# One searched round of 92 single steps, a second transpose bank, and FFN output in the FFN input's banks

## The chip, the cores and the metric

The kernel runs on one core of a Trainium2 chip. The metric is the device time in microseconds (us). The time of the kernel before is 358.19 us (median of 2 runs, 357.36 to 359.02). PE is the TensorE, DVE the VectorE, ACT the ScalarE, POOL the GpSimd, SP the engine that issues most DMA here. A program on one core has no second die to compare with, so "slow" below only means that a run was over 1.5% above the fastest run of the same kernel.

## The reference, cut to what matters

A recurrent attention (state 40x40 for each of 4x8 heads, 768 steps) feeds a feed-forward layer with a squared ReLU.

```
for t in range(S):
    y[:, :, t] = einsum('bhd,bhde->bhe', rt, state)
    Sa = einsum('bhde,bhe->bhd', state, at)
    state = state * wt[:, :, None, :] - einsum('bhd,bhe->bhde', Sa, bt) + einsum('bhd,bhe->bhde', vt, kt)
x = y.transpose(0, 2, 1, 3).reshape(B * S, H * D)        # 3072 x 320
h = x @ w_in;  r = maximum(h, 0);  out = (r * r) @ w_out   # 320 -> 2048 -> 320
```

The kernel works in 12 chunks of 64 time steps. In each round of its main loop it does three things at once: the recurrence of chunk c, the preparation (logs, scalings, transposes) of chunk c+1, and the feed-forward layer of chunks c-1 and c-2.

## The kernel before: the parts that matter

The kernel before shares out eight banks of PSUM like this: `hp` two (FFN input and cumulative sums), `acc` two (one buffer), `sq` two (one buffer), `tr` **one** (all transposes), `op2` one (FFN output). A helper makes the transposes and copies them out of PSUM at once. Most other steps too are a product with its evacuation right behind it:

```
def transposes(srcs, dst, eng):
    trp = ps.tile([128, 8, 128], BF16, name="trp", tag="tr", bufs=1)
    for i, s in enumerate(srcs):
        nc.tensor.transpose(out=trp[:, i, :], in_=s, identity=IDb[:])
    if eng == "act":
        nc.scalar.activation(out=dst, in_=trp[:], func=ACTF.Copy)
    else:
        nc.vector.tensor_copy(out=dst, in_=trp[:])

def g0(self, bp):          # product, then its evacuation on ACT
    self.pairs(self.accm[bp], self.PNT[bp], self.vm_of(self.VM, bp), not self.first)
    self.evac_m(bp, self.G0)
```

The main loop, cut (`cur` is chunk c, `nxt` c+1, `prv` c-1, `old` c-2):

```
for c in range(NCH):
    cur.a_s0(0); cur.pn(1); cur.g0(0)
    nxt.cs(0); nxt.cs(1); nxt.gamp(); prv.t_x()
    ...
    old.ffn_out(1, 0); cur.m(0); nxt.scale_b(); nxt.scale_k(); nxt.decays(); old.ffn_out(1, 1)
    cur.state(0); cur.t_vm(0, "dve"); nxt.scale_a()
    ...
    prv.ffn_in(0); prv.ffn_in(1); cur.a_s0(1); cur.cx(0); cur.g0(1)
    prv.ffn_in(2); nxt.t_r(); cur.t_s(0, nxt); cur.m(1); nxt.spread()
    prv.ffn_in(3); prv.ffn_in(4); cur.state(1); cur.t_vm(1, "dve"); nxt.t_kb(0)
    prv.ffn_in(5); cur.r_s0(0); cur.cx(1); cur.y(0); nxt.t_kb(1)
    prv.ffn_in(6); nxt.t_a(); cur.t_s(1, nxt); prv.ffn_in(7)
    ...
```

The program is scheduled by hand: each engine gets its own instructions in the order of this text and does not leave it.

Of the kernel before, what the change touches and what calls it, by code (L numbers as in the profile page):

```python
# [14 lines left out]
def kernel(  # L15
# [109 lines left out]
    def load(c, nat):  # L125
        for key, src in (("W", w), ("B", b), ("K", k), ("A", a)):
            t_ = ld.tile([128, NI, D], FP32, name=f"N{key}", tag=f"N{key}")
            for b2 in range(2):
                nc.sync.dma_start(out=t_[64 * b2:64 * b2 + 64], in_=src_view(src, c, b2))  # L129
            nat[key] = t_  # L130
# [17 lines left out]
    def transposes(srcs, dst, eng):  # L148
        trp = ps.tile([128, 8, 128], BF16, name="trp", tag="tr", bufs=1)
        for i, s in enumerate(srcs):  # L150
            nc.tensor.transpose(out=trp[:, i, :], in_=s, identity=IDb[:])  # L151
        if eng == "act":
            nc.scalar.activation(out=dst, in_=trp[:], func=ACTF.Copy)  # L153
        else:
            nc.vector.tensor_copy(out=dst, in_=trp[:])  # L155
# [5 lines left out]
    class Chunk:  # L161


        def __init__(self, c):
            self.c, self.nat = c, {}
            self.first, self.last = c == 0, c == NCH - 1
            i = c % 2
            self.Ap, self.Rp, self.Kp, self.Bp = Aps[i], Rps[i], Kps[i], Bps[i]
            self.VM = VMs[i]
            self.G0, self.Y = G0s[i], Ys[i]  # L170
            self.S, self.Sn = Ss[1 - i], Ss[i]
            self.ST, self.STn = {}, {}
            self.PNT, self.CXT, self.VMT, self.accm, self.accy = {}, {}, {}, {}, {}


        def ln(self):
# [4 lines left out]
            self.CSE = pr.tile([128, W_], FP32, name="CSE", tag="CSE", bufs=1)  # L181
            self.GAMI = pr.tile([128, W_], FP32, name="GAMI", tag="GAMI", bufs=1)

        def cs(self, j):
            cs = ps.tile([128, 512], FP32, name="cs", tag="hp", bufs=2)
            sl = slice(320 * j, 320 * j + 320)
            nc.tensor.matmul(out=cs[:, 0:320], lhsT=UTI[:], rhs=self.lnW[:, sl],  # L187
                             start=True, stop=True)
            nc.scalar.activation(out=self.GAMI[:, sl], in_=cs[:, 0:320], func=ACTF.Exp,  # L189
                                 scale=-1.0)  # L190
            nc.vector.tensor_tensor(out=self.CSE[:, sl], in0=cs[:, 0:320],  # L191
                                    in1=self.lnW[:, sl], op=ALU.subtract)
# [5 lines left out]
        def decays(self):  # L198
            GAMb = pr.tile([128, W_], BF16, name="GAMb", tag="GAMb", bufs=1)
            nc.gpsimd.tensor_tensor(out=GAMb[:], in0=self.GAMP[:],  # L200
# [3 lines left out]
            self.GLr = pr.tile([128, 4, 2, 160], BF16, name="GLr", tag="GLr")  # L204
            self.gld = dr.tile([2, W_], BF16, name="gld", tag="gld")
            for b2 in range(2):
                nc.gpsimd.dma_start(out=self.gld[b2:b2 + 1, :],
                                    in_=GAMb[64 * b2 + 63:64 * b2 + 64, :])

        def spread(self):  # L210
            for b2 in range(2):
# [13 lines left out]
        def scale_b(self):  # L225
            self.KB = pr.tile([128, 2, NI, 64], BF16, name="KB", tag="KB")
            self.scale("B", self.Bp, self.GAMI)
# [4 lines left out]
        def scale_k(self):  # L232
            self.scale("K", self.Kp, self.GAMI)
            for b2 in range(2):
# [7 lines left out]
        def t_r(self):  # L242
            self.RT = pr.tile([128, NG, 128], BF16, name="RT", tag="RT")
            transposes([self.Rp[:, 2 * g:2 * g + 2, :] for g in range(NG)], self.RT[:], "act")

        def t_kb(self, b2):
            if b2 == 0:
                self.KBT = pr.tile([128, 2, NG, 128], BF16, name="KBT", tag="KBT")
            transposes([self.KB[:, b2, 2 * g:2 * g + 2, :] for g in range(NG)],
                       self.KBT[:, b2], "act")  # L250

        def t_a(self):
            self.AT = pr.tile([128, NG, 128], BF16, name="AT", tag="AT")
            transposes([self.Ap[:, 2 * g:2 * g + 2, :] for g in range(NG)], self.AT[:], "act")


        def squares(self, lhs_of, rhs_of, dst):
# [3 lines left out]
            for g in range(4):  # L261
                for b2 in range(2):
                    for x in range(2):
                        mm(sq[:, x, g, b2, :], lhs_of(g, b2, 64 * x), rhs_of(g, b2, 64 * x),
                           True)
            nc.vector.tensor_tensor(  # L266
                out=dst[:].rearrange("s x g b t -> s (x g b) t"),
                in0=sq[:].rearrange("s x g b t -> s (x g b) t"),
                in1=MASK[:].to_broadcast([128, 16, L]), op=ALU.mult)

        def pn(self, bp):
            self.PNT[bp] = wk.tile([128, 2, 4, 2, L], BF16, name="PNT", tag="PNT")
            self.squares(lambda g, b2, r0: self.KBT[r0:r0 + D, b2, 4 * bp + g, :],
                         lambda g, b2, r0: self.AT[r0:r0 + D, 4 * bp + g,
                                                   64 * b2:64 * b2 + 64],
                         self.PNT[bp])

        def cx(self, bp):
            self.CXT[bp] = wk.tile([128, 2, 4, 2, L], BF16, name="CXT", tag="CXT")
            self.squares(lambda g, b2, r0: self.VMT[bp][r0:r0 + D, g, b2, :],  # L280
                         lambda g, b2, r0: self.RT[r0:r0 + D, 4 * bp + g,
                                                   64 * b2:64 * b2 + 64],
                         self.CXT[bp])
# [4 lines left out]
        def a_s0(self, bp):  # L288

            acc = self.accm[bp] = self.new_acc()  # L290
# [9 lines left out]
        def r_s0(self, bp):  # L300

            acc = self.accy[bp] = self.new_acc()
# [24 lines left out]
        def evac_m(self, bp, dst):  # L327
            for b2 in range(2):
                rows = slice(64 * b2, 64 * b2 + 64)
                src = self.accm[bp][rows, :, 0:320].rearrange(  # L330
# [6 lines left out]
        def g0(self, bp):  # L337
            self.pairs(self.accm[bp], self.PNT[bp], self.vm_of(self.VM, bp), not self.first)
            self.evac_m(bp, self.G0)

        def m(self, bp):
            self.pairs(self.accm[bp], self.PNT[bp], self.vm_of(self.G0, bp), True)
            self.evac_m(bp, self.VM)

        def state(self, bp):
# [3 lines left out]
            accs = self.new_acc()  # L349
# [5 lines left out]
            for z in range(2):  # L355
                for b2 in range(2):
                    for q in range(2):
# [4 lines left out]
                           kb[:, 2 * bp + q, :, z, 0:D], self.first and g == 0)  # L362
            for p in range(2):
# [10 lines left out]
        def t_s(self, bp, nxt):  # L374
            if self.last:
                return
            trs = ps.tile([128, 4, 2, 64], BF16, name="trs", tag="tr", bufs=1)
            for g in range(4):
                b2, q = divmod(g, 2)
                nc.tensor.transpose(out=trs[:, g].rearrange("s p d -> s (p d)"),  # L380
                                    in_=self.Sn[:, bp, b2, q].rearrange("s z e -> s (z e)"),
                                    identity=IDb[:])

            ST = nxt.ST[bp] = wk.tile([128, 2, 2, 2, D], BF16, name="ST", tag=f"ST{bp}")
            nc.vector.tensor_copy(out=ST[:].rearrange("s b q p d -> s (b q) p d"),  # L385
                                  in_=trs[:, :, :, 0:D])

        def t_vm(self, bp, eng):
            self.VMT[bp] = wk.tile([128, 4, 2, 128], BF16, name="VMT", tag="VMT")
            transposes([self.VM[:, b2, 8 * bp + 2 * g:8 * bp + 2 * g + 2, :]  # L390
                        for g in range(4) for b2 in range(2)],
                       self.VMT[bp][:].rearrange("s g b t -> s (g b) t"), eng)

        def y(self, bp):
            accy = self.accy[bp]
            self.pairs(accy, self.CXT[bp], self.kb_of(bp), not self.first)
            for b2 in range(2):
# [8 lines left out]
        def t_x(self):  # L406
            self.XT = wk.tile([128, 3, 2, 128], BF16, name="XT", tag="XT")
            trx = ps.tile([128, 3, 2, 128], BF16, name="trx", tag="tr", bufs=1)
            for g in range(3):
                for bp in range(2):  # L410
                    at = 320 * bp + 128 * g
                    nc.tensor.transpose(out=trx[:, g, bp, :], in_=self.Y[:, at:at + 128],
                                        identity=IDb[:])
            nc.scalar.activation(out=self.XT[:], in_=trx[:], func=ACTF.Copy)
            self.Gt = wk.tile([128, NJ, 256], BF16, name="Gt", tag="Gt")

        def ffn_in(self, jj):
            hp = ps.tile([128, 2, 256], FP32, name="hp", tag="hp", bufs=2)
            for u in range(2):
                j = 2 * jj + u  # L420
                for g in range(3):
# [3 lines left out]
                        start=(g == 0), stop=(g == 2))  # L425
            if jj % 2 == 0:
                self.hs = wk.tile([128, 4, 256], BF16, name="hs", tag="hs", bufs=2)
            u = 2 * (jj % 2)
            nc.scalar.activation(out=self.hs[:, u:u + 2], in_=hp[:], func=ACTF.Relu)  # L429
            if jj % 2:  # L430
                nc.vector.tensor_tensor(out=self.Gt[:, 2 * jj - 2:2 * jj + 2, :],  # L431
                                        in0=self.hs[:], in1=self.hs[:], op=ALU.mult)

        def ffn_out(self, bp, part):
            if part == 0:
                self.op = ps.tile([128, DM], FP32, name="op2", tag="op2", bufs=1)
            for j in range(8 * part, 8 * part + 8):
                nc.tensor.matmul(  # L438
                    out=self.op[:], lhsT=self.Gt[:, j, 128 * bp:128 * bp + 128],
                    rhs=WOUT[:, j, :], start=(j == 0), stop=(j == NJ - 1))  # L440
            if part == 0:
                return
            osb = wk.tile([128, DM], FP32, name="osb", tag="osb")
            nc.scalar.activation(out=osb[:], in_=self.op[:], func=ACTF.Copy)
# [5 lines left out]
    class Nothing:  # L450
        def __getattr__(self, name):
            return lambda *args: None

    with tc.manual_schedule():
# [126 lines left out]
```

## Time and profile before

| | before |
|---|---|
| span of the profiled run | 356.3 us |
| a steady round (chunk 2 to 10) | 26.30 us |
| in it: PE / DVE / ACT / POOL busy | 20.26 / 17.79 / 15.46 / 9.59 us |
| start until the first A product of round 1 | 56.91 us |

The profile's page of the kernel before, the busy time of PE to POOL (with share of the span and number of instructions), and the chain of work that ended last by engine:

```profile
PE 254.8 (72%) x3656; PEld 202.7 (57%) x3656; DVE 217.2 (61%) x354; ACT 188.2 (53%) x325; POOL 118.6 (33%) x143
...
PE 39%; ACT 26%; DVE 14%; DMA 7%; issue 7%; SPq 5%; ACTq 0%; DVEq 0%
```

The view by windows, two steady rounds of the kernel before. The columns are the length, the busy time of each engine with its instructions, PE's granted clock, the DMA share and GB/s:

```profile
137.00:163.30 26.30, 20.27 (x312) 16.22 (x310) 17.79 (x29) 15.47 (x27) 9.59 (x11) 1.00 0.84 107
163.30:189.60 26.30, 20.26 (x312) 16.23 (x310) 17.79 (x29) 15.46 (x27) 9.59 (x11) 1.00 0.80 107
```

No engine is busy for the whole round, and the granted clock is full. The rounds are alike to a hundredth of a us, so one can look at one. PE's timeline in it (start, length, instructions; in brackets the idle time before, and what ended it), cut to the transposes:

```profile
174.47 0.61 PE L151 MATMUL trp<-IDb,Rp_86 128*128 128x128 bf16 x8
176.47 0.38 PE L380 MATMUL trs<-IDb,S_97 128*128 128x128 bf16 x4 [1.40 <-ACT RT L153]
...
178.84 0.61 PE L151 MATMUL trp<-IDb,VM_93 128*128 128x128 bf16 x8
181.09 0.61 PE L151 MATMUL trp<-IDb,KB 128*128 128x128 bf16 x8 [1.63 <-DVE VMT L155]
...
183.06 0.61 PE L151 MATMUL trp<-IDb,KB 128*128 128x128 bf16 x8
...
184.78 0.61 PE L151 MATMUL trp<-IDb,Ap_84 128*128 128x128 bf16 x8 [0.46 <-ACT KBT L153]
186.50 0.38 PE L380 MATMUL trs<-IDb,S_97 128*128 128x128 bf16 x4 [1.11 <-ACT AT L153]
```

Four of these groups, the ones with a bracket, stand idle until the copy of the group before them has ended. The waits of PE, summed over the steady rounds (who waited, for whom; us in total, times, longest):

```profile
PE trp L151 <- DVE VMT L155: 14.7, 9, 1.6
PE trs L380 <- ACT RT L153: 12.6, 9, 1.4
PE trs L380 <- ACT AT L153: 10.0, 9, 1.1
PE trp L151 <- ACT KBT L153: 4.1, 9, 0.5
PE acc L158 <- DVE Y_99 L402: 3.7, 5, 0.7
PE acc L158 <- ACT VM_92 L332: 3.5, 5, 0.7
...
```

The first four lines are the one transpose bank: (14.7+12.6+10.0+4.1)/9 = 4.6 us a round.

### The profile page before, as it was taken

To read this page: it belongs to the slowest core of one execution; us is meant where nothing else is said; L and a number is where in the kernel's file an instruction comes from. 1 tells how busy PE (TensorE), PEld (TensorE's weight loads), DVE (VectorE), ACT (ScalarE), POOL (GpSimd) and SP (SyncE) were. 2 spreads that over 40 slices of the span, in tenths; PEclk is the share of its full clock that TensorE was granted. 3 is DMA by queue.
4 is the path that set the end of the run, shared out by engine and by line. 5 is a ranking of instruction groups with operands and counts; after the bars stand their busy time and mean duration, and the time that the engine had idled before them with its cause. 6 is when DMAs were issued, how large, how long until landed. Compare 5 with 4: busy or idle time off the path is not lost.

```text
span 356.3 us, 8782 instructions
## 1 busy us (share of the span) xinstructions
PE 254.8 (72%) x3656; PEld 202.7 (57%) x3656; DVE 217.2 (61%) x354; ACT 188.2 (53%) x325; POOL 118.6 (33%) x143
## 2 busy tenths in 40 slices
PE   1344366677778768769769769768868868779994
PEld 0233355565666656656656656656755756657773
DVE  1626546756856856756757657658658658655720
ACT  2243233554654764764655655655655655655561
POOL 7563440640640640640640640541541532200000
PEclk9998556899999999999999999999999999999999
DMA  9999998991892892991991990991991991401011
GB/s 104 148 192 154 155 177 100 122 153 22 109 160 46 121 151 42 126 163 28 134 153 28 138 155 22 149 135 36 158 132 35 157 125 45 86 2 29 11 37 37
DMA packets 162199, 36.31 MB, mean 102 GB/s; under 512 B 152712, under 2 KB 158144, under 8 KB 162160
## 3 DMA queue, kind: packets, MB, share of 16 engines
q1 hardware_dynamic: 107520, 25.96, 43.0%
q0 software_dynamic: 54640, 9.79, 34.2%
q8 instruction: 28, 0.46, 0.6%
q14 instruction: 11, 0.09, 0.1%
HBM read 32.03 MB, written 3.96 MB: 101 GB/s over the span
## 4 chain that ended last, share of the span: by engine, by line
PE 39%; ACT 26%; DVE 14%; DMA 7%; issue 7%; SPq 5%; ACTq 0%; DVEq 0%
PE acc L158 10%; PE hp L422 9%; DMA NK<-in_k_dram 7%; PE trp L151 7%; SPq L129 5%; ACT hs L429 4%; PE sq L158 3%; ACT KBT L153 3%; ACT AT L153 3%; ACT G_94 L332 3%; ACT RT L153 3%; PE trs L380 2%; DVE VMT L155 2%; ACT VM_92 L332 2%; DVE CSE L191 2%
## 5 line engine op out<-in xcount | busy, mean ns | idle before, releaser
L422 PE MATMUL hp<-XT,WIN 128*128 128x256 bf16 x576 | 74.9, 274 | 0.1
L429 ACT ACTIVATE hs<-hp 128x512 bf16<-128x512 f32 x96 | 56.0, 595 | 32.7 <-PE hp L422 31.7
L431 DVE TENSOR_TENSOR Gt<-hs 128x1024 bf16<-128x1024 bf16 x48 | 33.1, 690 | 57.9 <-ACT hs L429 57.9
L200 POOL TENSOR_TENSOR GAMb<-GAMP,NW 128x640 bf16<-128x640 f32 x12 | 19.3, 1611 | 134.6 <-issue 117.7
L422 PEld LDWEIGHTS <-WIN 128*128 128x128 bf16 x576 | 53.6, 99 | 6.0 <-issue 0.6
L153 ACT ACTIVATE KBT<-trp 128x1024 bf16<-128x1024 bf16 x24 | 24.6, 1023 | 41.0 <-PE trp L151 41.0
L438 PEld LDWEIGHTS <-Gt 128*128 128x128 bf16 x384 | 35.8, 98 | 12.5 <-issue 0.9
L266 DVE TENSOR_TENSOR PNT<-sq,MASK 128x1024 bf16<-128x1024 f32 x24 | 29.3, 1223 | 17.4 <-PE sq L158 10.2
L151 PE MATMUL trp<-IDb,KB 128*128 128x128 bf16 x192 | 16.2, 233 | 24.1 <-DVE VMT L155 15.6
L266 DVE TENSOR_TENSOR CXT<-sq,MASK 128x1024 bf16<-128x1024 f32 x24 | 29.2, 1218 | 1.6 <-PE sq L158 1.6
L151 PEld LDWEIGHTS <-KB 128*128 128x128 bf16 x192 | 13.4, 105 | 25.9 <-issue 25.9
L187 PE MATMUL cs<-lnW,UTI 128*128 128x320 f32 x48 | 19.2, 530 | 7.9 <-ACT lnW L178 7.9
L385 DVE COPY ST<-trs 128x320 bf16<-128x320 bf16 x22 | 7.1, 325 | 26.0 <-PE trs L380 26.0
L212 POOL DMA_DIRECT2D GLr<-gld x24 | 19.9, 846 | 4.4 <-DVE Gt L431 1.9
L158 PEld LDWEIGHTS <-PNT 128*128 128x128 bf16 x384 | 18.4, 104 | 3.2 <-issue 1.1
L191 DVE TENSOR_TENSOR CSE<-cs,lnW 128x320 f32<-128x320 f32 x24 | 10.8, 486 | 13.8 <-ACT GAMI L189 13.8
L155 DVE COPY VMT<-trp 128x1024 bf16<-128x1024 bf16 x24 | 16.6, 692 | 3.2 <-PE trp L151 2.5
L332 ACT ACTIVATE G_94<-acc 64x320 bf16<-64x320 f32 x24 | 10.4, 431 | 15.3 <-PE acc L158 15.2
L140 POOL DMA_DIRECT2D VM_93<-in_v_dram x12 | 10.2, 863 | 22.0 <-PE trp L151 22.0
L140 POOL DMA_DIRECT2D VM_92<-in_v_dram x12 | 10.0, 841 | 21.1 <-PE trp L151 20.9
L187 PEld LDWEIGHTS cs<-lnW,UTI 128*128 128x128 f32 x48 | 9.8, 226 | 10.5 <-ACT lnW L178 7.9
L380 PE MATMUL trs<-IDb,S_96 128*128 128x128 bf16 x48 | 5.0, 231 | 14.8 <-ACT RT L153 8.1
(144 smaller groups left out, 538.2 us busy)
## 6 DMA issues: line engine op xcount, KB each, us to landing
NW<-in_w_dram SPq DMA_DIRECT2D x24, 160.0 KB, 6.3
NB<-in_b_dram SPq DMA_DIRECT2D x24, 160.0 KB, 7.1
NK<-in_k_dram SPq DMA_DIRECT2D x24, 160.0 KB, 5.9
NA<-in_a_dram SPq DMA_DIRECT2D x24, 160.0 KB, 5.1
out_dram<-osb SPq DMA_DIRECT2D x48, 80.0 KB, 2.1
GLr<-gld POOLq DMA_DIRECT2D x24, 130.0 KB, 6.2
KB<-Bp_90 SPq DMA_DIRECT2D x12, 128.0 KB, 2.3
KB<-Kp_88 SPq DMA_DIRECT2D x12, 128.0 KB, 2.3
```

The costliest lines, as they stand in the source:

```text
L140: nc.gpsimd.dma_start(out=VMs[c % 2][row:row + 64, b2, :, 0:D], in_=src_view(v, c, b2))
L151: nc.tensor.transpose(out=trp[:, i, :], in_=s, identity=IDb[:])
L153: nc.scalar.activation(out=dst, in_=trp[:], func=ACTF.Copy)
L155: nc.vector.tensor_copy(out=dst, in_=trp[:])
L158: nc.tensor.matmul(out=out, lhsT=lhsT, rhs=rhs, start=start, stop=True, skip_group_check=True)
L187: nc.tensor.matmul(out=cs[:, 0:320], lhsT=UTI[:], rhs=self.lnW[:, sl], start=True, stop=True)
L266: nc.vector.tensor_tensor(out=dst[:].rearrange("s x g b t -> s (x g b) t"), in0=sq[:].rearrange("s x g b t -> s (x g b) t"), in1=MASK[:].t ...
L332: nc.scalar.activation(out=dst[rows, b2, 8 * bp:8 * bp + 8, 0:D].rearrange("s (z g) d -> s z g d", z=2), in_=src[:, :, :, b2, :], func=ACT ...
L422: nc.tensor.matmul(out=hp[:, u, :], lhsT=WIN[:, g, j * 128:(j + 1) * 128], rhs=self.XT[:, g].rearrange("f b t -> f (b t)"), start=(g == 0) ...
L429: nc.scalar.activation(out=self.hs[:, u:u + 2], in_=hp[:], func=ACTF.Relu)
L431: nc.vector.tensor_tensor(out=self.Gt[:, 2 * jj - 2:2 * jj + 2, :], in0=self.hs[:], in1=self.hs[:], op=ALU.mult)
L438: nc.tensor.matmul(out=self.op[:], lhsT=self.Gt[:, j, 128 * bp:128 * bp + 128], rhs=WOUT[:, j, :], start=(j == 0), stop=(j == NJ - 1))
```

## The change

The intent: let PE never wait. An offline search orders one fixed round, in which a product and its evacuation are separate steps. Each step says how many chunks ahead of the round it works. Two banks go to the transposes. To pay for the second one, FFN output gives up its own bank and takes turns in the two of FFN input. Start and end of the kernel come from the same round, with the steps of chunks that don't exist left out. The core of the diff, with cuts marked:

```
-    def transposes(srcs, dst, eng):
-        trp = ps.tile([128, 8, 128], BF16, name="trp", tag="tr", bufs=1)
+    def transposes(srcs):
+        trp = ps.tile([128, 8, 128], BF16, name="trp", tag="tr", bufs=2)
         for i, s in enumerate(srcs):
             nc.tensor.transpose(out=trp[:, i, :], in_=s, identity=IDb[:])
-        if eng == "act": ...
+        return trp
 ...
         def g0(self, bp):
-            self.pairs(self.accm[bp], ...)
+            self.pairs(self.ps["m", bp], ...)
+
+        def g0e(self, bp):
             self.evac_m(bp, self.G0)
 ...                                     (likewise for every product)
-                self.op = ps.tile([128, DM], FP32, name="op2", tag="op2", bufs=1)
+                self.ps["o", bp] = ps.tile([128, 512], FP32, name="op2", tag="hp", bufs=2)
 ...
+    ROUND = """
+        t_x -1, a_s0 0 +0, t_xe -1, cs 0 +1, cs 1 +1, gami 0 +1, g0 0 +0, clear_m +1,
+        cse 0 +1, gami 1 +1, pn 1 +0, ffn_in 0 -1, g0e 0 +0, cse 1 +1, t_r +1, m 0 +0,
+        ffn_ine 0 -1, ffn_in 1 -1, pne 1 +0, scale_b +1, me 0 +0, ffn_in 2 -1, scale_k +1,
+        t_vm 0 +0, ffn_ine 1 -1, state 0 +0, ffn_in 3 -1, ffn_ine 2 -1, t_vme 0 +0,
+        state_e 0 +0, ffn_in 4 -1, cx 0 +0, a_s0 1 +0, g0 1 +0, t_re +1, load_v +1,
+        ffn_ine 3 -1, gamp +1, ffn_sq 1 -1, stack_b +1, decays +1, g0e 1 +0,
+        ffn_out 1 0 -2, t_s 0 +0, cxe 0 +0, m 1 +0, ffn_ine 4 -1, ffn_sq 3 -1, stack_k +1,
+        load +2, gather +1, ffn_out 1 1 -2, me 1 +0, t_kb 0 +1, state 1 +0, ffn_in 5 -1,
+        scale_a +1, t_se 0 +0, t_vm 1 +0, state_e 1 +0, t_kbe 0 +1, t_kb 1 +1,
+        ffn_oute 1 -2, ffn_ine 5 -1, t_kbe 1 +1, r_s0 0 +0, t_vme 1 +0, ffn_in 6 -1,
+        y 0 +0, ffn_in 7 -1, ffn_sq 5 -1, cx 1 +0, ffn_ine 6 -1, ye 0 +0, ffn_ine 7 -1,
+        t_a +1, t_ae +1, r_s0 1 +0, ffn_out 0 0 -1, cxe 1 +0, y 1 +0, ln +2, pn 0 +1,
+        ffn_sq 7 -1, ye 1 +0, ffn_out 0 1 -1, pne 0 +1, ffn_oute 0 -1, t_s 1 +0, spread +1,
+        load_r +2, t_se 1 +0
+    """
 ...
+        for rnd in range(-lead, NCH - lag):
+            for name, args, ahead in steps:
+                if 0 <= rnd + ahead < NCH:
+                    getattr(ch[rnd + ahead], name)(*args)
```

An `e` at the end of a step's name is the evacuation of that product; `cs` has two, `gami` on ACT and `cse` on DVE. `ffn_sq` squares two evacuated FFN tiles on DVE.

## The prediction

> **What bounds it now.** In the page, PE is busiest (72% of 356.3 us), then DVE 61%, ACT 53%. The table of windows shows a steady state: every round from 84.4 to 321 us takes 26.30 us, with PE busy 20.26, DVE 17.79, ACT 15.47, POOL 9.6 us, clock 1.00. PE's timeline in 163-190 us shows where PE stands still, each round at the same places: 1.63 us before the KB transposes (released by DVE's VMT copy), 1.40 us before the state transposes (released by ACT's RT copy), 1.11 us the same (AT copy), 0.46 us (KBT copy), 0.7 us each before acc work (released by Y and VM evacuations) and about 0.3 us more behind G. The first four, 4.6 us, are the single transpose bank: PE may not transpose until the previous copy has ended. The rest is order: product, evacuation and the next product stand next to each other in the program. So no engine bounds the round; in-order waiting does. The Trainium skill (Perfetto Trace Analysis, Optimization Strategy) says that a gap that keeps repeating on the engine that should be full can mean too little PSUM for the next tile; this trace agrees.
>
> **What changes.** No arithmetic is added or removed. The FFN output gives up its own bank and shares the two of FFN input and cs; the transposes get two banks. Every evacuation stands some steps after its product, with other PE work between.
>
> **Cost of the new round.** From start-to-start times in uninterrupted stretches of the PE timeline: FFN in 8x0.65-0.75 us, FFN out 4x1.09-1.18, six groups of transposes 0.44, t_x 0.34, t_s 2x0.22, cs 1.15, squares 4x0.33, pairs 6x0.30, state 2x0.55, s0 products 4x0.15. Sum about 19.0 to 19.7 us: an estimate of PE's floor. DVE needs about 17.7 us, of which 1.35 us is a Kp scaling stretched (1827 instead of 482 ns) while POOL forms GAMb; ACT 15.6. Walking the 95 steps by hand with these durations, I find PE almost never waiting: acc, sq, hp and transpose banks come free 0.1 to 3 us ahead of need. The tightest are me 0 before t_vm 0, me 1 before state 1, ye 0 before the second r_s0, and load_r, which ends about 1 us before t_r. I add about 0.8 us for what the walk misses: 20.2 us a round.
>
> DMA: a round moves 2.82 MB, and the DMA queues are busy for 17 of the 26.3 us at about 150 GB/s. At 20.2 us that is 85% full, so landings slip, but loads are issued earlier in the round.
>
> **Sum.** The head (WIN, WOUT and chunk loads, DMA share above 1, clock 0.50 at 40-58 us) gains only about 3 us; the first full round starts near 54 us and takes about 24. Then 9x20.2, the last round without next-chunk work 15, the tail 17.5-18, and 2 us outside the span: about 296 us.
>
> Predicted 296 us, range 285 to 314. Faster by over 2%: 0.97; within 2%: 0.02; slower: 0.01.
>
> **What would show it.** Steady rounds of 19.5-21 us in the windows; PE over 90% busy in them; the waits of transposes for copies gone (4.6 us a round to under 1); the chain of waits mostly PE, ACT's share falling from 26% to about 10%; operation counts and mean durations unchanged.
>
> **What would make it wrong.** Loads landing late (r before t_r, K before its scaling), which would make DMA the bound near 22 us; DVE stalls from POOL now hitting a critical step; PE running FFN groups slower when interleaved; FFN out, which holds one of two shared banks, blocking FFN in.

## The result, and the profile after

The changed kernel takes 290.95 us (median of 2 runs, 290.48 to 291.41). The ratio to the kernel before is 0.8123 (95% interval 0.8024 to 0.8221): faster by 19%. Ratios here are the mean time of one kernel's fast runs over that of the other's fast runs of the same rounds, so they are not quite the ratio of the medians quoted.

The profile's page of the changed kernel, the lines that answer to those of before:

```profile
PE 251.4 (87%) x3656; PEld 203.8 (70%) x3656; DVE 207.8 (72%) x354; ACT 189.1 (65%) x325; POOL 117.0 (40%) x143
...
PE 66%; DMA 18%; SPq 5%; issue 4%; POOL 2%; DVE 2%; ACT 2%; POOLq 0%; ACTq 0%; DVEq 0%
```

The counts and the busy times are nearly those of before; only the idle time between them has gone. In the chain of waits ACT's share fell from 26% to 2%. The view by windows, two steady rounds of the changed kernel:

```profile
95.36:115.41 20.05, 20.05 (x313) 16.49 (x311) 16.94 (x29) 15.57 (x28) 10.22 (x12) 1.00 1.12 136
115.41:135.46 20.05, 20.05 (x313) 16.50 (x311) 16.94 (x29) 15.57 (x28) 9.11 (x11) 1.00 1.07 147
```

The round is 20.05 us and PE is recorded as busy in all of it. That alone proves little: the Trainium skill ("Perfetto Trace Analysis", Identifying the Most-Contended Engine) warns that busy time of pipelined matmuls is a poor measure of how near the limit one is, and names better ones, among them the share of time in weight loads. That went from 57% to 70% of the span, and in the steady round from 62% (16.22 of 26.30 us) to 82% (16.49 of 20.05). Whether PE's work bounds the round was left to the experiments. PE's timeline of the second of these rounds, the same transposes in their new places:

```profile
117.91 0.61 PE L150 MATMUL trp<-IDb,Rp_87 128*128 128x128 bf16 x8
...
124.23 0.39 PE L150 MATMUL trp<-IDb,S_96 128*128 128x128 bf16 x4
...
125.83 0.61 PE L150 MATMUL trp<-IDb,KB 128*128 128x128 bf16 x8
...
127.49 0.61 PE L150 MATMUL trp<-IDb,VM_92 128*128 128x128 bf16 x8
127.94 0.61 PE L150 MATMUL trp<-IDb,KB 128*128 128x128 bf16 x8
...
130.77 0.62 PE L150 MATMUL trp<-IDb,Ap_85 128*128 128x128 bf16 x8
...
134.49 0.39 PE L150 MATMUL trp<-IDb,S_96 128*128 128x128 bf16 x4
```

No bracket is left. That does not rule out short waits: a product is recorded as some 0.2 us long, although the next one starts sooner, and two waits of 0.16 and 0.06 us in e8 (below) have no bracket either. Over all steady rounds the view of PE's waits has one line:

```profile
PE trp L150 <- DMA Rp_86<-in_r_dram: 0.8, 2, 0.5
```

In two of these rounds the r of the next chunk landed late. Cut at the same events (first A product of a round, last transposes of Y), the spans compare like this; each line is a difference of start times in PE's timelines:

| stretch | before, us | after, us | gained, us |
|---|---|---|---|
| start until round 1 | 56.91 | 53.41 | 3.5 |
| round 1 | 29.22 | 21.59 | 7.6 |
| rounds 2 to 10 | 236.69 (9 x 26.30) | 181.58 (9 x 20.18) | 55.1 |
| round 11 | 15.54 | 15.01 | 0.5 |
| the last chunk's FFN | 17.94 | 18.11 | -0.2 |

The steady rounds give 55.1 of 66.6 us. The first two lines are less sure than the others, because they differ from run to run: the granted clock between 40 us and the first copy of the transposed Y was 0.99 in this profile and 0.61 in e4, the same kernel. What the page of "Perfetto Trace Analysis" (the Trainium skill, Optimizing Tensor Performance, Matmuls) advises in general, to rotate independent products through different banks so that evacuations overlap the next products, is what the trace shows here, with 4.6 us of such waits a round before and none after.

### The profile page after: what moved, and what is told of

The parts are those of the page before. It is cut to its first block, busy times and chain, and to the rows that moved or that the text cites. A ratio compares the mean times of both kernels' runs of the same rounds, so it can differ in the third digit from the quotient of the medians.

```text
span 289.7 us, 8759 instructions
## 1 busy us (share of the span) xinstructions
PE 251.4 (87%) x3656; PEld 203.8 (70%) x3656; DVE 207.8 (72%) x354; ACT 189.1 (65%) x325; POOL 117.0 (40%) x143
## 4 chain that ended last, share of the span: by engine, by line
PE 66%; DMA 18%; SPq 5%; issue 4%; POOL 2%; DVE 2%; ACT 2%; POOLq 0%; ACTq 0%; DVEq 0%
PE hp L483 20%; PE acc L160 12%; PE trp L150 11%; DMA NK<-in_k_dram 7%; DMA Rp_86<-in_r_dram 5%; DMA NW<-in_w_dram 5%; SPq L129 4%; PE sq L160 4%; PE cs L198 4%; DMA gld<-GAMb 1%; PE op_4969 L508 1%; PE op_4529 L508 1%; PE op_3625 L508 1%; PE op_2269 L508 1%; PE op_1817 L508 1%
## 5 line engine op out<-in xcount | busy, mean ns | idle before, releaser
L483 PEld LDWEIGHTS <-WIN 128*128 128x128 bf16 x576 | 52.0, 98 | 8.2 <-issue 1.6
L220 POOL TENSOR_TENSOR GAMb<-GAMP,NW 128x640 bf16<-128x640 f32 x12 | 18.5, 1542 | 91.2 <-issue 78.8
L500 DVE TENSOR_TENSOR Gt<-hs 128x1024 bf16<-128x1024 bf16 x48 | 37.9, 790 | 8.8 <-ACT hs L493 8.1
L508 PEld LDWEIGHTS <-Gt 128*128 128x128 bf16 x384 | 34.6, 98 | 12.6
L234 POOL DMA_DIRECT2D GLr<-gld x24 | 19.8, 826 | 30.2 <-DMA gld<-GAMb 12.6
L211 DVE TENSOR_TENSOR CSE<-cs,lnW 128x320 f32<-128x320 f32 x24 | 11.8, 492 | 17.4 <-ACT GAMI L204 17.0
L160 PEld LDWEIGHTS <-PNT 128*128 128x128 bf16 x384 | 19.1, 104 | 6.4 <-issue 4.2
L418 DVE TENSOR_TENSOR S_96<-acc,GLr 40x320 bf16<-40x320 f32 x24 | 11.7, 486 | 9.6 <-PE acc L160 9.5
L160 PE MATMUL sq<-RT,VMT 40*128 40x64 bf16 x384 | 10.2, 195 | 6.6 <-DVE VMT L157 6.6
L204 ACT ACTIVATE GAMI<-cs 128x320 f32<-128x320 f32 x24 | 10.5, 437 | 8.3 <-PE cs L198 7.3
L160 PEld LDWEIGHTS <-VMT 40*128 40x128 bf16 x384 | 7.3, 97 | 11.6 <-DVE VMT L157 6.8
```

What stands on the lines that cost most here:

```text
L160: nc.tensor.matmul(out=out, lhsT=lhsT, rhs=rhs, start=start, stop=True, skip_group_check=True)
L220: nc.gpsimd.tensor_tensor(out=self.GAMb[:], in0=self.GAMP[:], in1=self.nat["W"][:].rearrange("p h e -> p (h e)"), op=ALU.mult)
L234: nc.gpsimd.dma_start(out=self.GLr[0:64 + D, :, b2, :], in_=self.gld[b2:b2 + 1, :].to_broadcast([64 + D, W_]).rearrange("s (g x) -> s g x" ...
L483: nc.tensor.matmul(out=hp[:, u, :], lhsT=WIN[:, g, j * 128:(j + 1) * 128], rhs=self.XT[:, g].rearrange("f b t -> f (b t)"), start=(g == 0) ...
L500: nc.vector.tensor_tensor(out=self.Gt[:, 2 * jj - 2:2 * jj + 2, :], in0=hs[:], in1=hs[:], op=ALU.mult)
L508: nc.tensor.matmul(out=op_[:, 0:DM], lhsT=self.Gt[:, j, 128 * bp:128 * bp + 128], rhs=WOUT[:, j, :], start=(j == 0), stop=(j == NJ - 1))
```

## The experiments

All runs of one group were on one chip, next to runs of the kernel before. Runs of one kernel spread by several us (the changed kernel gave 287.6 to 293.3 us in one group), and in the profiled runs mostly in the start: in the profiled run of e4 the second copy of the transposed Y came at 77.6 us, against 75.1 us in the first profile of the changed kernel, with plain rounds of 20.05 us in both. So the steady round is the sharper measure. It is read as the distance between ACT's copies of the transposed Y from round to round.

| run | what | steady round, us | time, us (median) |
|---|---|---|---|
| before | | 26.30 | 358.19 |
| changed | | 20.05 | 290.95 |
| e1 | old order, new banks | 22.37 | 312.19 |
| e2 | new order, old banks | 22.94 | 318.11 (its one fast run) |
| e3 | changed, every evacuation behind its product | 23.16, some 23.8 to 24.8 | 330.59 |
| e4 | changed again | 20.05 | 292.55 (287.63 fast) |
| e5 | changed, sums in float32r | 19.71 | 289.94 |
| e6 | before, sums in float32r | 26.30 | 357.89 |
| e7 | changed, without most loads of r and v | 20.05 | 288.79 |
| e8 | changed, one more copy on ACT | 20.26 | 290.57 |
| e9 | changed, one step moved on DVE | 21.75 | 310.28 |
| e10 | changed, only ACT's evacuations moved | 20.69, two of 23.9, one of 21.6 | 305.07 |
| e11 | e5 with the order fitted to it | 19.28 | 283.34 |

The theory: before, in-order waiting bounds the round; afterwards PE's own work does. Banks and order were each supposed to give about half. The rivals were that one of the two does it all, that only PE's order matters, and that DMA or the evacuations bind at 20 us.

### The yardstick

e4 is the changed kernel as it is, next to e1 to e3.

> The changed kernel itself on the same chip, as the yardstick for the other three: 290 to 292 us, ratio about 0.812.

Measured: 292.55 us median of 4 runs; rounds of 20.05 us.

### Banks alone, order alone

e1 is the kernel before with the new banks:

```
-        trp = ps.tile([128, 8, 128], BF16, name="trp", tag="tr", bufs=1)
+        trp = ps.tile([128, 8, 128], BF16, name="trp", tag="tr", bufs=2)
 (likewise trs and trx)
-    self.op = ps.tile([128, DM], FP32, name="op2", tag="op2", bufs=1)
+    self.op = ps.tile([128, 512], FP32, name="op2", tag="hp", bufs=2)[:, 0:DM]
```

> The old order of steps, but two transpose banks and FFN output in the shared FFN banks. Theory (banks and order each give about half): PE's waits of transposes for copies, 4.6 us a round before, fall under 1.5 us, but other in-order waits (squares for the VMT copy, acc work for evacuations) keep the round at about 22.5 to 23.5 us; 315 to 332 us. Rival 1 (the order does it all, banks are a side matter): over 350 us. Rival 2 (the banks do it all): under 300 us.

Measured: 312.19 us (311.33 to 313.55, 4 runs), ratio 0.8764 (0.8729 to 0.8800). The round is 22.37 us, 3.93 less, at the short end of what was expected; the total was 3 us below the expected range. PE's waits in eight steady rounds of e1:

```profile
PE acc L158 <- DVE Y L402: 5.9, 8, 0.7
PE op L438 <- DVE CSE L191: 3.7, 8, 0.5
PE sq L158 <- DVE VMT L155: 3.2, 8, 0.4
PE acc L158 <- ACT VM L332: 2.8, 8, 0.3
```

No transposes wait any more, so the four lines of before were the bank. What remains is (5.9+3.7+3.2+2.8)/8 = 1.95 us a round. The second line, 0.46 us of it, is a price of the shared bank: FFN output now waits for the reader of the sums that had the bank before. The rest is order.

e2 is the changed kernel with the old banks. With one bank a copy must stand before the next transposes in the text, so four copies move up; PE's order stays.

```
-        trp = ps.tile(..., name="trp", tag="tr", bufs=2)
+        trp = ps.tile(..., name="trp", tag="tr", bufs=1)
-        ... name="op2", tag="hp", bufs=2)
+        ... name="op2", tag="op2", bufs=1)
 ROUND: t_re before t_vm 0; t_se 0 before t_kb 0; t_kbe 0 before t_vm 1; t_vme 1 before t_kb 1
```

> The new order on PE, but one transpose bank and an own FFN output bank as before; four copies moved up so that each stands before the next transposes, as one bank demands. Theory (each about half): about 0.8 us lost before t_vm 0, 0.85 before the second KB transposes, 1 before t_x, so 22 to 23.5 us a round, 308 to 325 us. Rival 1 (order alone suffices): within 1% of 291. Rival 2 (banks are all): near 345 or more.

Measured: 318.11 us in its one fast run; the other three took 323.31 to 325.92. The round is 22.94 us, 2.9 above the changed kernel. PE's waits over six rounds of e2:

```profile
PE trp L150 <- DVE ST L439: 4.9, 6, 0.8
PE trp L150 <- DVE VMT L157: 4.7, 6, 0.8
PE trp L150 <- ACT RT L155: 4.6, 6, 0.8
```

These are the three places that were expected, with sizes of 0.8 us each. (The view leaves out 0.1 to 0.2 us of each: from start to start they cost 0.93 to 0.97 us, 2.8 of the 2.9.) So both rivals fall: banks alone give 3.9 us a round, order with the old banks 3.4, and both together 6.25, somewhat less than the sum. The second transpose bank and the shared FFN bank could not be told apart, because a second transpose bank with the own FFN output bank would need nine banks, one more than the kernel shares out. The record says most of it all the same: PE never waited for the FFN output's bank before, and sharing it cost 0.46 us a round in e1, so in the old order the gain of the banks is that of the second transpose bank. For the new order it stays open.

### Product and evacuation apart

e3 keeps the new banks and PE's new order, and puts each evacuation right behind its product in the text (`t_x, t_xe, a_s0 0, cs 0, gami 0, cse 0, cs 1, ...`), which changes only the order in which ACT and DVE work.

> New banks and the new order of products on PE, but each evacuation put right behind its product, so that ACT and DVE work in the order in which PE produces. Theory: urgent evacuations then stand behind ones that can wait (the first M evacuation behind the RT copy, about 1 us), so 1 to 2 us a round are lost: 302 to 315 us. Rival (only PE's order and the banks matter): 289 to 294 us.

Measured: 330.59 us (328.74 to 331.37), ratio 0.926. That is far worse than expected, and even worse than the old order with the new banks (e1). Two of its rounds took 24.8 us at a mean granted clock of 0.93, so they are not read; the plain rounds of 23.16 us ran at 1.00. So PE's order is not what makes the new round good, without the order of the evacuations. DVE's timeline of e3 shows a first-FFN squaring with 2.23 us of idle time before it, and PE's shows who pays:

```profile
179.62 0.69 DVE L500 TENSOR_TENSOR Gt<-hs 128x1024 bf16<-128x1024 bf16 x1 [2.23 <-ACT hs L493]
...
182.58 0.41 PE L160 MATMUL sq<-RT,VMT 40*128 40x64 bf16 x16 [1.12 <-DVE VMT L157]
```

My expectation had looked only at ACT (the M evacuation behind the RT copy). Two more runs told the engines apart.

e9 moves one step on DVE; a comparison of the two programs showed PE, ACT, POOL and SP with the same instructions in the same order.

```
-  ... pne 1, scale_b, scale_k, t_vme 0, state_e 0, ffn_sq 1, ...     (DVE's order)
+  ... pne 1, ffn_sq 1, scale_b, scale_k, t_vme 0, state_e 0, ...
```

> The changed kernel with one step moved on DVE alone: the first squaring of the FFN stands before the two scalings (B, K) instead of after the state evacuation; PE and ACT keep their order. Theory (an evacuation that must wait for ACT blocks all DVE work behind it): DVE idles about 1.6 us for ACT, the VMT copy and the state evacuation come about 2 us late, PE waits at the first CXT squares and at the second A product: round 21.3 to 21.8 us against 20.05. Rival (DVE's 3 us of idle time a round absorb it): under 20.3 us.

Measured: 310.28 us (306.61 to 313.76), ratio 0.8657 (0.8607 to 0.8707); the round is 21.75 us. The profiled run is the slow one of the four (some of its rounds are longer), but at full granted clock in its steady part, and its plain rounds are alike to 0.01 us. DVE's and PE's timelines of e9 in one round:

```profile
130.55 0.69 DVE L500 TENSOR_TENSOR Gt<-hs 128x1024 bf16<-128x1024 bf16 x1 [1.63 <-ACT hs L493]
131.16 0.89 DVE L242 TENSOR_TENSOR Bp<-NB,GAMI 128x320 bf16<-128x320 f32 x2
131.96 0.89 DVE L242 TENSOR_TENSOR Kp<-NK,GAMI 128x320 bf16<-128x320 f32 x2
132.76 0.68 DVE L157 COPY VMT<-trp 128x1024 bf16<-128x1024 bf16 x1
...
133.51 0.41 PE L160 MATMUL sq<-RT,VMT 40*128 40x64 bf16 x16 [0.97 <-DVE VMT L157]
134.40 0.32 PE L160 MATMUL acc<-ST,AT 40*128 40x80 bf16 x8 [0.49 <-DVE S L418]
```

As expected, both in place and in size: DVE waits 1.63 us for ACT at a step that nobody needs soon, with two scalings behind it whose inputs are ready, and then hands the delay to PE. One step in the wrong place costs 1.7 us a round, although DVE has 3.1 us of idle time in a round of 20.05. The Trainium skill ("TensorE: Matmul & The Clock Gate", the table at its head) states that the queues of ScalarE and VectorE are strict first in, first out; this trace agrees, with the scalings that stand still for 1.63 us.

e10 moves only ACT's evacuations behind their products; DVE and PE keep their order.

> The changed kernel with the evacuations of ACT alone put right behind their products; DVE and PE keep their order. Theory (what the run with all evacuations moved lost came from DVE's queue, ACT has about 0.75 us of room before each urgent copy): 20.2 to 20.7 us a round. Rival (ACT's queue made the loss): above 22 us.

Measured: 305.07 us (301.68 to 305.93), ratio 0.8528. The plain round is 20.69 us, as expected. But two rounds took 23.9 us, which was not expected. PE's waits in e10, cut to two lines, say why:

```profile
PE trp L150 <- DMA Rp<-in_r_dram: 5.8, 3, 3.1
PE trp L150 <- ACT VM L374: 1.8, 8, 0.2
...
```

The r load came late by 3.1 us in one of these rounds and by 2.0 in the other, which also had a mean granted clock of only 0.93; a third late r made a round of 21.6 us. ACT now makes the decay exponentials (`gamp`) after the second G evacuation; POOL's queue holds the decays, the gather, the spread and then the r load, one behind the other. That the later `gamp` made r late is argued from this order and was not tested by itself. So of the 3.1 us a round that e3 lost, ACT's order made about 0.6; if the parts add, the rest of 2.5 lies with DVE's order, of which e9 shows 1.7.

### What bounds the round of 20.05 us

e7 leaves out the loads of r and v from chunk 4 on; the results are wrong.

```
 def load_r(c):
+    if c >= 4: return      (likewise load_v)
```

> The changed kernel without the loads of r and v from chunk 4 on (wrong results on purpose; 0.65 of 2.82 MB a round less, head untouched). Theory (PE bound): rounds stay at 20.05 us, only the rounds that waited for a late r lose their extra 0.5 us; 0 to 1.5 us less in all. Rival (DMA bound): rounds fall to 17 to 19 us, 10 us or more less.

Measured: 288.79 us (288.16 to 291.17), ratio 0.8089. One steady round of e7, by windows:

```profile
100.00:120.05 20.05, 20.05 (x311) 16.50 (x310) 16.93 (x29) 15.56 (x29) 6.16 (x7) 1.00 0.69 124
```

The DMA share (the time of all packets over that of the 16 DMA engines, which can pass 1) falls from about 1.1 to 0.69 and the round stays at 20.05 us. Nine rounds from the second on are within 0.01 us, so the two late ones have gone. DMA does not bind in the steady part. The bytes fell less than expected, to 124 GB/s against 136 and 147 in the two rounds above; the 23% of the expectation (0.65 of 2.82 MB) did not come out.

e5 and e6 give the cumulative sums of the logs the type float32r, in the changed kernel and in the kernel before:

```
+    UTR = gl.tile([128, 128], mybir.dt.float32r, name="UTR")
+    nc.vector.tensor_copy(out=UTR[:], in_=UTI[:])
-            self.lnW = pr.tile([128, W_], FP32, ...)
+            self.lnW = pr.tile([128, W_], mybir.dt.float32r, ...)
-            nc.tensor.matmul(out=cs[:, 0:320], lhsT=UTI[:], ...)
+            nc.tensor.matmul(out=cs[:, 0:320], lhsT=UTR[:], ...)
```

> The changed kernel with the cumulative-sum products of the logs (1.19 us of PE a round[...]) in one-pass float32r: about 0.85 us of PE work less a round, nothing else changed. Theory (PE's own work bounds the round now): the round falls from 20.05 to 19.2 to 19.4 us, the time by 8 to 10 us against the changed kernel. Rival (DMA or the evacuations bind at 20 us too): the round stays above 19.8 us.

> The same cut of PE work in the kernel before. Theory (waiting in order bounds its round, PE's work does not): the sums stand beside the G evacuation on ACT, which ends at the same time, so the round of 26.30 us falls by 0.2 us at most and the time by under 1%. Rival (PE's work binds there too): 25.4 us a round, 9 us less.

Both results are correct. In PE's timeline the two sums advance PE by 0.41 us instead of 1.19 (start of the sums to start of the next product), 0.78 us less a round. e6: 357.89 us, ratio 1.0009 (0.9968 to 1.0051), round 26.30 us. The kernel before does not notice the cut, and PE's waits in five rounds of e6, cut to one line, show where it went:

```profile
PE acc L160 <- ACT VM L334: 7.3, 5, 1.5
```

This wait was 0.7 us in the kernel before. The time saved at the sums has become a longer wait for ACT's next M evacuation. So at this place ACT's queue sets the pace; PE work that stands elsewhere in the round was not cut.

e5: 289.94 us (one of its four runs counts as slow), ratio 0.8072; the round is 19.71 us, 0.34 less. So neither the theory's number (19.2 to 19.4) nor the rival's (above 19.8) came out. PE's timeline of e5 shows where the rest went:

```profile
117.11 0.57 PE L200 MATMUL cs<-lnW,UTR 128*128 128x320 f32 x2
117.52 0.46 PE L162 MATMUL acc<-VM,PNT 128*128 128x80 bf16 x8
117.91 0.41 PE L162 MATMUL sq<-AT,KBT 40*128 40x64 bf16 x16
118.68 0.82 PE L485 MATMUL hp<-XT,WIN 128*128 128x256 bf16 x6 [0.36 <-DVE CSE L213]
```

The first FFN product comes earlier than before and finds its bank still being read by DVE's `cse`. The cut turned into a new wait.

e11 takes e5, puts the R transposes before that FFN product, and issues the r load before the spread:

```
-  pn 1 +0, ffn_in 0 -1, g0e 0 +0, cse 1 +1, t_r +1, m 0 +0, ...
+  pn 1 +0, t_r +1, ffn_in 0 -1, g0e 0 +0, cse 1 +1, m 0 +0, ...
-  t_s 1 +0, spread +1, load_r +2, t_se 1 +0
+  t_s 1 +0, load_r +2, spread +1, t_se 1 +0
```

> The changed kernel with the one-pass float32r sums, and the order fitted to it: the R transposes stand before the first FFN product, which in the run with float32r alone waited 0.36 us for its bank; and the r load is issued before the decay spread. Theory (the rest of the cut was lost to that bank wait): 19.3 us a round, no late r, 282 to 286 us. Rival (something else binds at 19.7 us): round 19.6 to 19.8 us.

Measured: correct; 283.34 us (280.43 to 285.01, 6 runs, the longest of them slow), ratio 0.7913 (0.7876 to 0.7949). One steady round of e11, by windows:

```profile
115.00:134.28 19.28, 19.28 (x312) 16.02 (x309) 16.70 (x30) 15.11 (x28) 9.48 (x11) 1.00 1.16 147
```

The round is 19.28 us, 0.77 less than 20.05: the whole cut of 0.78 us now arrives. All rounds from the second to the tenth are within 0.01 us, so no r came late. With PE work taken out, the round shrinks by just that much once the order fits. The new order was not run without float32r, but PE's timelines leave it no share in the gain: apart from the sums, every group of products advances PE by the same time as in the changed kernel, to about 0.01 us. That shows that PE's work bounds the round. e11 is also faster than both kernels (its ratio to the kernel before is 0.7913, that of the changed kernel 0.8123, and their intervals don't meet).

e8 adds a copy of 128x1024 on ACT before the fourth FFN evacuation:

```
+  idle_act +0,        nc.scalar.activation(out=SCR[:], in_=SCI[:], func=ACTF.Copy)
   ffn_ine 3 -1, gamp +1, ...
```

> The changed kernel with one idle copy of about 1 us added on ACT each round, in the middle, before the fourth FFN evacuation. ACT is busy only 15.6 of 20.05 us. Theory (PE bound, but the slack of each evacuation is small): the copy delays the second G evacuation and the products behind it, 0.5 to 0.9 us a round, 6 to 10 us in all. Rival (4.5 us of idle time on ACT absorb it): under 1 us in all.

Measured: 290.57 us (289.59 to 291.27), ratio 0.8117. The round is 20.26 us, 0.21 more; in the total time that is lost in the spread. ACT's timeline of e8 shows the copy and, further on, the second G evacuation; the FFN evacuation behind the copy and the decay exponentials stand in between:

```profile
120.95 1.07 ACT L448 ACTIVATE SCR<-SCI 128x1024 bf16<-128x1024 bf16 x1
...
123.00 0.87 ACT L377 ACTIVATE G<-acc 64x320 bf16<-64x320 f32 x2
```

The copy takes 0.95 us of ACT (120.95 until the next step at 121.90), and the round grows by 0.21. So some 0.74 us were absorbed. Against the changed kernel, PE starts FFN output 0.16 us late, as soon as the FFN evacuation behind the copy has ended and its bank is free, and the second product of G another 0.06 us late, after the G evacuation. So most of the loss was not where I expected it. My expectation of 0.5 to 0.9 us was too high, the rival's zero too low: this place in ACT's order has about three quarters of a microsecond of room.

## Why the prediction was right

The range, 285 to 314 us, holds the measured 290.95; 296 was 1.7% too high. Point by point:

- *In-order waiting bounds the kernel before, not an engine.* Supported: without arithmetic taken away, banks and order alone shorten the round (e1, e2), and 0.78 us less PE work at the sums left it at 26.30 us (e6). That no PE work anywhere in that round counts is not shown; PE has 39% of its chain of waits.
- *The one transpose bank costs 4.6 us a round.* Right as a mechanism: with the banks alone those four waits are gone (e1) and with the old banks they are back at three places (e2). The banks alone gave 3.9 us, because other waits came forward.
- *PE's floor 19.0 to 19.7 us, a round of 20.2.* Measured 20.05 in the plain rounds and 20.18 on average. From start to start, groups of the same kind with the same neighbours take the same time wherever they stand in the round, so 20.05 is PE's work in this order and not hidden waiting. The allowance of 0.8 us was meant for waits, and there are none in a plain round; it is luck that it matches about 0.7 us of work that the sum had left out (20.05 less the middle of 19.0 to 19.7). The timelines, before and then after, show what that work is:

```profile
188.56 0.32 PE L158 MATMUL acc<-S_96,RT 40*128 40x80 bf16 x8
188.71 0.40 PE L158 MATMUL sq<-AT,KBT 40*128 40x64 bf16 x16
...
131.33 0.32 PE L160 MATMUL acc<-S_97,RT 40*128 40x80 bf16 x8
131.58 1.26 PE L508 MATMUL op_2269<-WOUT,Gt 128*128 128x320 bf16 x8
```

  The eight state products, over 40 rows, advance PE by 0.15 us where squares, over 40 rows too, come next, and by 0.25 where a product over 128 rows comes next. The group before a 40-row group also takes 0.1 us more (six FFN products 0.75 instead of 0.66). The old order enters 40-row products four times a round, the new one seven times. By an estimate from these numbers the three more cost 0.6 us a round. The sum had used the old 0.15. An order that keeps them together was not run.
- *The counts and durations stay.* Right: PE 254.8 against 251.4 us busy with the same 3656 products. One duration moved. Before, POOL's decay product stretched a Kp scaling on DVE (1827 instead of 482 ns); now it stands beside the mask of CXT and stretches only the squaring behind it (1.17 instead of 0.69 us). The Trainium skill ("SBUF — State Buffer", Who interferes with whom) says that a DVE instruction with two inputs in SBUF contends with a GpSimd instruction that reads SBUF, and that one with a single SBUF input, outside the two-port modes, does not. The trace agrees: CXT, which reads one input from PSUM, keeps its 1.22 us beside POOL.
- *DMA at 85% will let landings slip.* Partly: r was late in two rounds, and rounds 2 to 10 took 181.58 instead of 9 x 20.05 = 180.45 us, 1.1 us in all. The margin of "about 1 us" for the r load was too generous. DMA did not bind (e7).
- *The sum.* Head 54 (measured 53.4), first full round 24 (21.6), nine rounds 181.8 (181.6), last round 15 (15.0), tail 17.5 to 18 (18.1), outside the span 2 (291.41 - 289.7 = 1.7). The mis-sized term is the first full round, by 2.4 us. That head and first round agree this well one by one is chance: in e7 and e8 the first copy of the transposed Y came at 45.5 and 44.1 us, against 54.2, and the second at 72.8 and 73.9, against 75.1. And these terms add up to about 294.5, not 296: I rounded up.
- *ACT's share of the chain of waits about 10%.* It fell further, to 2%.

What the prediction did not see, and the experiments did, is how much of the gain hangs on the order of the evacuations. It named the evacuations that stand some steps after their products as one feature among others. With PE's order and the banks right but the evacuations behind their products, the round is 23.16 us, so half of the gain of 6.25 us is lost, more through DVE than through ACT (e3, e9, e10).

## What to carry to other kernels

When no engine is full and the same gaps repeat, count the banks first, but then order each engine's queue by when its result is needed, not by when its input is made: an evacuation that waits for another engine holds up everything behind it, and here one such step on DVE cost 1.7 us in a round of 20, with 3 us of idle time on that engine. Once an engine is full, take work out of it and fit the order again: the same cut gave 0.34 us a round in the old order, 0.77 in the fitted one, and nothing at all in the kernel before, where it only made a wait longer. Test a claim of "bound by X" by removing work from X in both kernels, and by relieving its rivals.

## What the Trainium skill lacked or had wrong

- "Perfetto Trace Analysis" (Optimization Strategy) offers too little PSUM or SBUF as what a repeating gap can mean. Here that was 3.9 of the 6.25 us a round (e1); the order of the evacuation queues, on which it has no advice beyond making what blocks start sooner, loses 3.1 us a round by itself (e3 against the changed kernel).
- "TensorE: Matmul & The Clock Gate" gives no time for products in float32 or float32r, and no other page gives one for float32r. Two products of 128x128 with 128x320 advanced PE by 1.19 us in float32 and by 0.41 us in float32r (e5). The trace lists each product as two records in float32 and as one in float32r.
- The same page (Part 4) gives a PE transpose of 128x128 as about 275 ns in a kernel. Here one is recorded with 219 ns, but eight in a row advance PE by 0.44 us, 55 ns each; for planning PE's time the second number is the one that counts, and for transposes the page has no such rate.
- "TensorEngine Tiling (Array Packing)" gives no time for changing between products over 40 and over 128 rows. Here each change cost PE about 0.1 us, and the new order makes six more of them a round than the old one.
